# Last layer of a cross network: the sum of five output pairs made by an accumulating DMA onto seeded rows

## The chip, the cores and the metric

The kernel runs on one core of a Trainium2 chip. Its metric is the device time of one execution in microseconds (us), the median of repeated runs. Beside it stands one profiled execution, whose trace gives the start and length of every instruction. The engines are TensorE (PE; PEld is its weight load), VectorE (DVE), ScalarE (ACT), GpSimd (POOL) and SyncE (SP). SP, ACT and GpSimd can issue DMAs; a trailing q in a row (SPq, ACTq) means the engine's instruction queue.

## What is computed

```python
B, F, D, L = 4096, 26, 16, 6          # Din = 416
def reference(x0, ws, bs):            # x0: B x Din, ws: L x Din x Din, bs: L x Din, all bf16
    x = x0
    for l in range(ws.shape[0]):
        x = x0 * (x @ ws[l] + bs[l]) + x
    return x
```

Each of six layers multiplies the activations by a 416 x 416 matrix, adds a bias, multiplies by the first input x0 and adds the layer's own input x.

## The kernel before

Layers 0 to 4 work on transposed activations: features on the partitions (three full blocks of 128 in XM, the 32 that remain in XR, four groups of rows side by side), the 4096 rows along the free axis, in two halves s of 2048. For each tile TensorE sums in PSUM, ScalarE copies out and adds the bias (L146, L152), VectorE multiplies by x0 and adds x (L147, L148, L153, L154).

The last layer turns the roles round, so that its result comes out with rows on the partitions, as the output wants them. Its input is needed in that form too. XLrows holds it, 128 x 32 x 416: SP's DMA transposes (`xl_dmat`, L182) fill the 384 main columns, one for each half s and block of 128 features, as the tiles of layer 4 are finished; the 32 other columns go through scrR (L234) and two GpSimd copies (L235). X0rows holds x0 in the same form (L109).

The last layer has eight quads q (L269): q = 0 to 3 are in half s = 0, q = 4 to 7 in s = 1. A quad is four blocks of 128 rows, in two pairs h = 0 and 1; pair h has a PSUM tile of two blocks. `mm_q_full` (L281) gives 12 matmuls for a quad, `mm_q_rem` (L287, L290) the 32 remaining features and the bias. In odd quads but the last, the remainder comes last and closes both pairs together; in the others it comes first, and each pair closes with its own last matmul. PSUM has room for four such tiles.

For a pair, `ew_pair` (L293) copies PSUM into a t tile on ScalarE (L299), multiplies in place by X0rows on VectorE (L300), adds XLrows into an o tile on VectorE (L301) and stores 128 x 2 x 416 values, 208 KB, from SP (L302). The last quad's second pair is split into two single blocks, groups 2 and 3 (`ew_single`, L304 to L312), whose stores of 104 KB go out from ACT and from SP.

Two pools matter. t tiles come from `tpool`, four buffers used in turn (L41), by all layers; o tiles from `opool`, ten buffers (L42). An instruction that takes a buffer again waits for the last reader of what was in it, be that an engine or a DMA. Each engine runs its instructions in the order of its queue; a framework places the waits and may move an instruction forward or back in the queue when it builds the program. SP's queue carries, towards the end, the transposes into XLrows, then the output stores.

Of the kernel before, what the change touches and what calls it, by code (L numbers as in the profile page):

```python
# [10 lines left out]
ALU = mybir.AluOpType  # L11
BF16 = mybir.dt.bfloat16
# [4 lines left out]
def kernel(  # L17
# [7 lines left out]
    nc = tc.nc  # L25
    B, D = x0.shape
    L = ws.shape[0]
    P = 128
# [5 lines left out]
    CW = 512  # L34
# [6 lines left out]
    tpool = ctx.enter_context(tc.tile_pool(name="tpool", bufs=4))  # L41
    opool = ctx.enter_context(tc.tile_pool(name="opool", bufs=10))  # L42
# [3 lines left out]
    out_v = out.rearrange("(bt p) d -> p bt d", p=P)  # L46
# [12 lines left out]
    X0rows = big.tile([P, NBT, D], BF16)  # L59
    XLrows = big.tile([P, NBT, D], BF16)  # L60
# [117 lines left out]
    def new_pts():  # L178
        return [psum.tile([P, 2, CW], FP32, tag="ps", name=f"pt{h}") for h in range(2)]
# [89 lines left out]
    quads = [(s, i) for s in range(NS) for i in range(4)]  # L269
    NQ = len(quads)  # L270
# [7 lines left out]
    def mm_q_full(q, py, rem_first):  # L278
        for g in range(NG):
            for k in range(NK):  # L280
                nc.tensor.matmul(py[g // 2][:, g % 2, 0:D], lhsT=cur[:, k, q_cols(q, g)], rhs=WM[:, l, k, :],  # L281
                                 start=((not rem_first) and k == 0), stop=(rem_first and k == NK - 1))

    def mm_q_rem(q, py, rem_first):
        s, i = quads[q]
        for g in range(NG):
            nc.tensor.matmul(py[g // 2][:, g % 2, 0:D], lhsT=curR[32 * g:32 * g + 32, CW * s + 128 * i:CW * s + 128 * i + 128],  # L287
                             rhs=WR[32 * g:32 * g + 32, l, :], start=rem_first, stop=False, tile_position=(32 * g, 0))
        for g in range(NG):
            nc.tensor.matmul(py[g // 2][:, g % 2, 0:D], lhsT=ones[32 * g:32 * g + 1, :],  # L290
                             rhs=bLr[32 * g:32 * g + 1, :], start=False, stop=(not rem_first), tile_position=(32 * g, 0))

    def ew_pair(q, h, py):  # L293
        s, i = quads[q]
        b0 = 16 * s + 8 * h + i
        t = tpool.tile([P, 2 * CW], BF16, name="t")
        tv = t[:, 0:2 * D].rearrange("p (a d) -> p a d", a=2)
        o = opool.tile([P, 2, D], BF16, name="o")
        nc.scalar.copy(tv, py[h][:, :, 0:D])  # L299
        nc.vector.tensor_tensor(out=tv, in0=tv, in1=X0rows[:, b0:b0 + 5:4, :], op=ALU.mult)  # L300
        nc.vector.tensor_tensor(out=o[:], in0=tv, in1=XLrows[:, b0:b0 + 5:4, :], op=ALU.add)  # L301
        nc.sync.dma_start(out_v[:, b0:b0 + 5:4, :], o[:])  # L302

    def ew_single(q, g, py, eng):  # L304
        s, i = quads[q]
        b = 16 * s + 4 * g + i
        t = tpool.tile([P, 2 * CW], BF16, name="t")
        o = opool.tile([P, 2, D], BF16, name="o")
        nc.scalar.copy(t[:, 0:D], py[g // 2][:, g % 2, 0:D])
        nc.vector.tensor_tensor(out=t[:, 0:D], in0=t[:, 0:D], in1=X0rows[:, b, :], op=ALU.mult)  # L310
        nc.vector.tensor_tensor(out=o[:, 0, :], in0=t[:, 0:D], in1=XLrows[:, b, :], op=ALU.add)
        return lambda: eng.dma_start(out_v[:, b, :], o[:, 0, :])  # L312

    py = {0: new_pts()}
    mm_q_rem(0, py[0], True)
    for q in range(NQ):
        rem_first = (q % 2 == 0) or (q == NQ - 1)
        if q == NQ - 1:
            py[q] = new_pts()
            mm_q_rem(q, py[q], True)  # L320
        elif not rem_first:
            py[q] = new_pts()
        mm_q_full(q, py[q], rem_first)
        if not rem_first:
            mm_q_rem(q, py[q], False)
            if q + 1 < NQ - 1:
                py[q + 1] = new_pts()
                mm_q_rem(q + 1, py[q + 1], True)
        if q < NQ - 1:
            for h in range(2):  # L330
                ew_pair(q, h, py[q])
        else:
            ew_pair(q, 0, py[q])
            stores = [ew_single(q, 2, py[q], nc.scalar), ew_single(q, 3, py[q], nc.sync)]
            for st in stores:
                st()
# [30 lines left out]
```

## Time and profile before

| what | value |
|---|---|
| median of 3 runs | 135.62 us |
| the 3 runs | 134.5, 135.98, 135.62 us |
| the profiled execution's own time | 134.11 us |
| its span, first to last instruction | 132.3 us |
| mean granted TensorE clock | 0.993 |
| busy share of the span: PE, DVE, ACT, POOL | 94%, 80%, 63%, 5% |
| bytes read from and written to HBM | 6.23 MB, 3.41 MB |

The profiled execution's time is 1.8 us above its span (134.11 less 132.3), which is what lies around the first and the last instruction. A group's row names the line, engine, operation, output <- inputs, shape and count, then busy time in us and mean ns of one, then the engine's idle time before them and what ended it. A timeline row has start and length in us from the start of the span; a row with xN covers N such instructions.

### The profile page before, as it was taken

The numbers are of one execution on the slowest core, as the hardware profiler recorded it, in microseconds if no ns is written. First come the engines' busy times: TensorE is split into PE (matmuls) and PEld (weight loads), VectorE is DVE, ScalarE is ACT, GpSimd is POOL, SyncE is SP. The second block draws the span as 40 slices with busy tenths as digits, with TensorE's granted clock in tenths as the row PEclk, the third lists the DMA queues.
The fourth block names the chain that finished last, engine by engine and source line by source line (L and its number), as shares of the span: only waits on it lengthen the run. The fifth ranks groups of instructions, "written<-read, shape, count | busy, mean of one in ns | idle before, by whom it ended". The sixth has DMA issues, their size and how long they took to land.

```text
span 132.3 us, 2235 instructions
## 1 busy us (share of the span) xinstructions
PE 124.0 (94%) x847; PEld 51.5 (39%) x847; DVE 105.9 (80%) x180; ACT 83.1 (63%) x89; POOL 6.4 (5%) x18
## 2 busy tenths in 40 slices
PE   5799999999999999999999999999999999999920
PEld 2343343433334343434343434334434354554400
DVE  1013886989979898979898979898979999988990
ACT  0407484597849567848659756849565984584740
POOL 4011000420000000000000000000004100000000
PEclk9999999999999999999999999999999999999997
DMA  4999999999990000000000000000597899995453
GB/s 106 208 256 209 149 114 277 239 332 333 336 284 6 0 2 5 0 0 0 0 0 5 0 0 0 0 0 5 95 195 136 150 193 146 205 303 193 158 184 111
DMA packets 42095, 16.33 MB, mean 123 GB/s; under 512 B 30811, under 2 KB 42085, under 8 KB 42085
## 3 DMA queue, kind: packets, MB, share of 16 engines
q1 hardware_dynamic: 39272, 15.53, 52.5%
q10 hardware_dynamic: 2812, 0.67, 2.7%
q8 instruction: 6, 0.10, 0.3%
q14 instruction: 5, 0.03, 0.1%
HBM read 6.23 MB, written 3.41 MB: 73 GB/s over the span
## 4 chain that ended last, share of the span: by engine, by line
PE 83%; SPq 5%; DMA 3%; DVE 3%; issue 2%; ACT 1%; DVEq 0%
PE pt L159 48%; PE pt L281 10%; PE ph L193 9%; SPq L74 5%; PE pt L164 5%; PE pr L175 5%; DMA XM<-in_x_dram 3%; DVE t L300 2%; PE pr L170 2%; PE ph L210 2%; PE pt L287 1%; PE pt L290 1%; ACT t L299 1%; DVE o L301 1%; DVE t L310 0%
## 5 line engine op out<-in xcount | busy, mean ns | idle before, releaser
L159 PE MATMUL pt<-XM,WM 128*128 128x512 bf16 x288 | 65.1, 380 | 0.0
L146 ACT ACTIVATE t<-pt,bM 128x1024 bf16<-128x1024 f32 x48 | 49.6, 1115 | 19.6 <-PE pt L164 19.6
L147 DVE TENSOR_TENSOR t<-t,XM 128x1024 bf16<-128x1024 bf16 x60 | 41.7, 694 | 9.9 <-ACT t L146 9.3
L148 DVE TENSOR_TENSOR XM<-t,XM 128x1024 bf16<-128x1024 bf16 x60 | 41.7, 695 | 3.4
L159 PEld LDWEIGHTS <-WM 128*128 128x128 bf16 x288 | 26.8, 98 | 37.2 <-issue 7.2
L146 ACT ACTIVATE t<-ph,bM 128x1024 bf16<-128x1024 f32 x12 | 12.5, 1112 | 9.3 <-PE ph L210 9.3
L281 PE MATMUL pt<-WM,XM 128*128 128x416 bf16 x96 | 17.7, 340 | 0.0
L193 PE MATMUL ph<-XM,WM 128*128 128x512 bf16 x72 | 16.5, 379 | 1.0 <-DMA XM<-in_x_dram 0.8
L299 ACT CAST t<-pt 128x832 bf16<-128x832 f32 x15 | 12.2, 854 | 7.2 <-PE pt L290 5.2
L281 PEld LDWEIGHTS <-XM 128*128 128x128 bf16 x96 | 9.0, 98 | 8.4 <-issue 1.7
L193 PEld LDWEIGHTS <-WM 128*128 128x128 bf16 x72 | 6.8, 98 | 9.5 <-issue 2.0
L300 DVE TENSOR_TENSOR t<-t,X0rows 128x832 bf16<-128x832 bf16 x15 | 8.8, 585 | 0.9 <-ACT t L299 0.9
L301 DVE TENSOR_TENSOR o<-t,XLrows 128x832 bf16<-128x832 bf16 x15 | 8.9, 592 | 0.6
L152 ACT ACTIVATE t<-pr,bR 128x512 bf16<-128x512 f32 x10 | 6.5, 686 | 3.0 <-PE pr L175 2.6
L175 PE MATMUL pr<-XM,WM 128*32 128x512 bf16 x120 | 8.2, 379 | 0.0
L164 PE MATMUL pt<-XR,WR 32*128 32x512 bf16 x96 | 7.3, 379 | 0.0
L235 POOL COPY XLrows<-scrR 128x512 bf16<-128x512 bf16 x2 | 1.9, 962 | 73.8 <-DMA scrR<-XR 73.8
L154 DVE TENSOR_TENSOR XR<-t,XR 128x512 bf16<-128x512 bf16 x10 | 4.2, 423 | 0.7
L123 PE MATMUL wps<-warm 128*128 128x512 bf16 x8 | 3.3, 582 | 1.5 <-DVE dz L84 1.5
L96 ACT ACT_TABLE_LOAD x1 | 1.3, 1283 | 5.1 <-issue 5.1
L175 PEld LDWEIGHTS <-WM 128*32 128x32 bf16 x120 | 3.2, 97 | 2.6
L153 DVE TENSOR_TENSOR t<-t,XR 128x512 bf16<-128x512 bf16 x10 | 4.2, 416 | 0.0
(36 smaller groups left out, 29.7 us busy)
## 6 DMA issues: line engine op xcount, KB each, us to landing
X0rows<-in_x_dram SPq DMA_DIRECT2D x4, 832.0 KB, 11.3
out_dram<-o SPq DMA_DIRECT2D x15, 208.0 KB, 2.6
WM<-in_ws_dram SPq DMA_DIRECT2D x5, 312.0 KB
WR<-in_ws_dram SPq DMA_DIRECT2D x4, 130.0 KB, 4.2
WM<-in_ws_dram ACTq DMA_DIRECT2D x1, 312.0 KB
XM<-in_x_dram SPq DMA_TRANSPOSE x8, 5.0
xrem<-in_x_dram ACTq DMA_DIRECT2D x1, 128.0 KB, 5.8
xrem<-in_x_dram SPq DMA_DIRECT2D x1, 128.0 KB, 4.6
```

Source lines behind the costliest of these rows:

```text
L74: nc.sync.dma_start_transpose(out=XM[0][:, :, c0:c0 + CW], in_=x0[c0:c0 + CW, 0:NK * P])
L146: nc.scalar.activation(t[:], pt[:].rearrange("p a b -> p (a b)"), ACT.Identity, bias=bM[:, m, l:l + 1], scale=1.0)
L147: nc.vector.tensor_tensor(out=t[:], in0=t[:], in1=XM[0][:, m, c0:c0 + 2 * CW], op=ALU.mult)
L148: nc.vector.tensor_tensor(out=nxt[:, m, c0:c0 + 2 * CW], in0=t[:], in1=cur[:, m, c0:c0 + 2 * CW], op=ALU.add)
L159: nc.tensor.matmul(pts[g // 2][:, g % 2, :], lhsT=WM[:, l, k, 128 * m:128 * m + 128], rhs=cur[:, k, c0:c0 + CW], start=(first and k == 0), ...
L164: nc.tensor.matmul(pts[g // 2][:, g % 2, :], lhsT=WR[32 * g:32 * g + 32, l, 128 * m:128 * m + 128], rhs=curR[32 * g:32 * g + 32, CW * s:CW ...
L175: nc.tensor.matmul(pr[32 * g:32 * g + 32, :], lhsT=WM[:, l, k, NK * P:D], rhs=cur[:, k, c0:c0 + CW], start=False, stop=(k == NK - 1), tile ...
L193: nc.tensor.matmul(pt[m][:, gl, :], lhsT=WM[:, 0, k, 128 * m:128 * m + 128], rhs=cur[:, k, c0:c0 + CW], start=(k == 0), stop=False)
L281: nc.tensor.matmul(py[g // 2][:, g % 2, 0:D], lhsT=cur[:, k, q_cols(q, g)], rhs=WM[:, l, k, :], start=((not rem_first) and k == 0), stop=( ...
L299: nc.scalar.copy(tv, py[h][:, :, 0:D])
L300: nc.vector.tensor_tensor(out=tv, in0=tv, in1=X0rows[:, b0:b0 + 5:4, :], op=ALU.mult)
L301: nc.vector.tensor_tensor(out=o[:], in0=tv, in1=XLrows[:, b0:b0 + 5:4, :], op=ALU.add)
```

## The change

The five pairs (q, h) = (5, 0), (5, 1), (6, 0), (6, 1) and (7, 0) no longer get their add on VectorE. Their output rows are first filled with the layer's input: `seed_out` stores the pair's part of XLrows from SP, five stores, written in the code after the pairs of q = 3. When the pair's product t * X0rows is in the t tile, GpSimd issues a DMA from it that adds onto the output rows. Pair (7, 0) has its copy and multiply in two halves of 128 x 416 (`ew_split`). The other ten pairs and the two single blocks are as before. Matmuls, pools and the layers before are unchanged.

```diff
@@ ew_pair @@
         t = tpool.tile([P, 2 * CW], BF16, name="t")
         tv = t[:, 0:2 * D].rearrange("p (a d) -> p a d", a=2)
-        o = opool.tile([P, 2, D], BF16, name="o")
         nc.scalar.copy(tv, py[h][:, :, 0:D])
         nc.vector.tensor_tensor(out=tv, in0=tv, in1=X0rows[:, b0:b0 + 5:4, :], op=ALU.mult)
+        if (q, h) in by_dma:
+            nc.gpsimd.dma_start(out_v[:, b0:b0 + 5:4, :], tv, accum_op=ALU.add)
+            return
+        o = opool.tile([P, 2, D], BF16, name="o")
         nc.vector.tensor_tensor(out=o[:], in0=tv, in1=XLrows[:, b0:b0 + 5:4, :], op=ALU.add)
         nc.sync.dma_start(out_v[:, b0:b0 + 5:4, :], o[:])
+
+    def seed_out(q, h):
+        s, i = quads[q]
+        b0 = 16 * s + 8 * h + i
+        nc.sync.dma_start(out_v[:, b0:b0 + 5:4, :], XLrows[:, b0:b0 + 5:4, :])
+
+    def ew_split(q, h, py):
+        s, i = quads[q]
+        b0 = 16 * s + 8 * h + i
+        t = tpool.tile([P, 2 * CW], BF16, name="t")
+        for a in range(2):
+            nc.scalar.copy(t[:, a * D:a * D + D], py[h][:, a, 0:D])
+            nc.vector.tensor_tensor(out=t[:, a * D:a * D + D], in0=t[:, a * D:a * D + D], in1=X0rows[:, b0 + 4 * a, :], op=ALU.mult)
+        nc.gpsimd.dma_start(out_v[:, b0:b0 + 5:4, :], t[:, 0:2 * D].rearrange("p (a d) -> p a d", a=2), accum_op=ALU.add)
...
+    by_dma = [(q, h) for q in (NQ - 3, NQ - 2) for h in range(2)]
...
@@ loop over the quads @@
             for h in range(2):
                 ew_pair(q, h, py[q])
+            if q == NQ - 5:
+                for qq, h in by_dma + [(NQ - 1, 0)]:
+                    seed_out(qq, h)
         else:
-            ew_pair(q, 0, py[q])
+            ew_split(q, 0, py[q])
             stores = [ew_single(q, 2, py[q], nc.scalar), ew_single(q, 3, py[q], nc.sync)]
```

## The prediction

> **What bounds the kernel now.** I read the page first: its shares of the chain that ended last, then its groups and DMA rows. The chain is 83% TensorE, so up to the last layer every other engine hides behind the matmuls.
>
> ```profile
> span 132.3 us, 2235 instructions
> ...
> PE 83%; SPq 5%; DMA 3%; DVE 3%; issue 2%; ACT 1%; DVEq 0%
> ...
> L299 ACT CAST t<-pt 128x832 bf16<-128x832 f32 x15 | 12.2, 854 | 7.2 <-PE pt L290 5.2
> ...
> L300 DVE TENSOR_TENSOR t<-t,X0rows 128x832 bf16<-128x832 bf16 x15 | 8.8, 585 | 0.9 <-ACT t L299 0.9
> L301 DVE TENSOR_TENSOR o<-t,XLrows 128x832 bf16<-128x832 bf16 x15 | 8.9, 592 | 0.6
> ...
> L235 POOL COPY XLrows<-scrR 128x512 bf16<-128x512 bf16 x2 | 1.9, 962 | 73.8 <-DMA scrR<-XR 73.8
> ...
> out_dram<-o SPq DMA_DIRECT2D x15, 208.0 KB, 2.6
> ```
>
> The change touches only the end, so the chain in order of time comes next. TensorE carries it until 121.28; from there it goes ScalarE copy, then VectorE multiply, add, multiply, add to the end.
>
> ```profile
> 120.77 0.29 PE pt L287 x4
> 121.05 0.23 PE pt L290 x4
> 121.28 0.84 ACT t L299
> 122.13 0.02 issue
> 122.15 0.60 DVE t L300
> ```
>
> The timeline of the last 10 us has the times that everything below starts from (start, length).
>
> ```profile
> 121.27 2.37 ACT L299 CAST t<-pt 128x832 bf16<-128x832 f32 x3 [1.72 <-PE pt L290]
> ...
> 123.84 0.85 ACT L299 CAST t<-pt 128x832 bf16<-128x832 f32 x1 [0.20 <-PE pt L281]
> ...
> 125.46 0.85 ACT L299 CAST t<-pt 128x832 bf16<-128x832 f32 x1 [0.77 <-PE pt L281]
> ...
> 126.52 0.91 ACT L309 CAST t<-pt 128x416 bf16<-128x416 f32 x2 [0.20 <-PE pt L281]
> 126.67 0.58 DVE L300 TENSOR_TENSOR t<-t,X0rows 128x832 bf16<-128x832 bf16 x1
> 127.29 0.59 DVE L301 TENSOR_TENSOR o<-t,XLrows 128x832 bf16<-128x832 bf16 x1
> 127.80 0.65 DVE L310 TENSOR_TENSOR t<-t,X0rows 128x416 bf16<-128x416 bf16 x2
> 128.37 0.65 DVE L311 TENSOR_TENSOR o<-t,XLrows 128x416 bf16<-128x416 bf16 x2
> 128.77 0.38 ACTq L312 DMA_DIRECT2D out_dram<-o  x1
> 129.05 0.35 SPq L312 DMA_DIRECT2D out_dram<-o  x1
> ```
>
> The reader is to see that VectorE runs about one 1.13 us pair step after another while ScalarE has already finished (127.43). VectorE is late by some 0.8 us at the very end, and no more: with no adds ahead of them, the single multiplies could start when the last copies end. The last store, issued at 129.05, lands 1.8 us later (its own row), at 130.85, and the span ends 1.45 us after that.
>
> **The change part by part.** I write L for the time from the end of a multiply to the landing of its accumulating DMA, and g for the part of it in which GpSimd is occupied with the issue, since GpSimd issues the five one after the other.
>
> *Removed:* five adds of 592 ns on VectorE (2.96 us) and five SP stores. Of the 2.96 us only the lateness at the end is on the path. Without waits of any other kind, the last copy ends at 127.43, the multiply (368 ns) at 127.82, the add (368 ns, starting 0.07 later as in the rows) at 128.26, and SP stores at 128.29 instead of 129.05: a gain of 0.76 us. That is the ceiling of the change.
>
> *Added, seeds:* five SP stores of 208 KB from XLrows. In the built order they stand after the first two output stores, and the first waits for the last transposes into XLrows. The last of these is issued at 109.77 and a transpose of XLrows lands after 4.4 us, so at 114.2. Five issues at the slow pace of 0.757 us (the longest L302 row) end at 118.0; at 3.4 us (the slowest landing) the last lands by 121.4. Behind them wait the q1 to q3 stores, ready from 113.2 on; SP clears them at 0.45 us each (L302 at 115) before 122. The o pool has ten buffers, so VectorE waits for none of this. Cost 0; cover: the first accumulating DMA isn't ready before 122.74, and the first seed lands at about 117.6. If that cover of 5 us is gone, each us late is a us on the GpSimd queue.
>
> *Added, waits:* this decides. The t pool has four buffers. The pairs q5h0, q5h1, q6h0, q6h1 now hold one each until their DMA has landed, not until an add has read them. The built order shows the result: ScalarE's first q7h0 copy waits for the DMA of q5h0, the copy of group 2 for that of q5h1, the copy of group 3 for that of q6h0. Behind these copies stand all later ScalarE work (with its last store) and VectorE's last three multiplies and two adds.
>
> *L:* the trace has no GpSimd-issued DMA and no accumulating one, so both parts are bounded by the nearest rows. g: at least an SP issue, 0.37; at most, as an assumption, one 128x512 GpSimd copy, 0.96 (L235). The landing: at least a plain 208 KB store on a quiet queue, 2.1 (L302 at 123.4); at most a load followed by a store, since the destination must be read, then written: 4.6 (128 KB, xrem) + 2.1 = 6.7. So L lies between 2.47 and 7.66. I take 0.96 for g, because the one kind of GpSimd work seen near here has that length, and 3.4 for the landing: the slowest L302 store, when two 208 KB transfers lay in line, is nearest to one that moves the bytes twice. L = 4.36.
>
> *The sum with L = 4.36.* Multiplies of q5h0, q5h1, q6h0, q6h1 end at 122.74, 123.50, 124.25, 125.30 (copies end at 122.12, 122.88, 123.64, 124.69, and the adds between are gone). GpSimd starts at 122.78, 123.74, 124.70, 125.66; the DMAs land at 127.14, 128.10, 129.06, 130.02. ScalarE's q7h0 copy, free to run at 125.46 before, now starts at 127.19; its two halves take 0.91 (the L309 row, same shape), to 128.10; the second half's multiply ends at 128.49. GpSimd issues the fifth DMA at 128.54; it lands at 132.90. Meanwhile group 3's copy waits until 129.11, ends at 129.62, its multiply at 130.01, its add at 130.45, its store is issued at 130.48 and lands at 132.28. The later of the two, 132.90, plus 1.45 is 134.35: +2.05 on the span. L counts twice on this path, once in the wait and once in the last DMA: with the other terms kept, its change is 2L - 6.67, and that of group 3's store is L - 2.93.
>
> The profiled execution took 134.11 us and would take 136.2; the median of the three runs is 135.62, 1.5 us above it. On the median: 135.62 + 2.05 = 137.7 us.
>
> **A rule against a row.** Beside the two GpSimd copies of 101.04 to 102.95 two VectorE instructions took 0.91 and 1.09 us where the others of their lines took 0.69, so GpSimd work can slow VectorE; were the five issues to do so at the same rate, it would cost 0.1 to 0.2 us on a multiply of 0.37. In my sum the fourth issue ends at 126.62 and the multiplies on the path run after 127.7, so the term is 0 either way; with the quick landing below it would eat that much of the gain. The Trainium skill, SBUF — State Buffer, section "Who interferes with whom", says that a two-input VectorE instruction collides with a GpSimd instruction that reads SBUF and not with one that only writes, as descriptor generation does; by it this term is 0 in every case, and no run here shows it.
> The Trainium skill, DMA: Bandwidth & Descriptors, section "Anatomy of one DMA", fits a GpSimd-issued DMA as 2.0 us plus bytes over 436 GB/s: an estimate of 2.5 us for 208 KB, by which the sum would be -0.7 us; it speaks of plain copies, and the reading of the destination is not in it.
>
> **The rivals.**
> *Quick landing (other side, not slower).* L near its low end, 2.5: q5h0's DMA lands at 125.2, before the copy wants its buffer at 125.46; nobody waits; the fifth DMA, issued at 126.8, lands at 129.3, the last store at 130.1. That is the ceiling, -0.76 us: 134.9. For it: plain stores at this place land in 2.1. Against it: nothing plain reads its destination. It decides below L = 2.93, where group 3's path breaks even (the other does at 3.34); up to L = 3.8 the loss, 2L - 6.67 = 0.93, stays within what can be measured (136.6).
> *Slow accumulate.* L at 6 to 7.66: the copy starts at 128.8 to 130.5, and the last DMA, issued some 1.35 later, lands at 136.2 to 139.5: +5.3 to +8.7, 140.9 to 144.3. For it: loads in this trace take 4.6 us and more. Against it: those loads ran at the crowded start, and the queues near 125 are only half busy.
> *Seeds late.* The accumulating DMAs wait for their seeds. This decides once the first seed lands after 122.74. For it: the seeds wait for the transposes, which SP issues slowly (3.13 us for the last). Against it: the 5 us of cover. One us beyond the cover adds one to the forecast: 138.7.
>
> **How the numbers follow.** Forecast (L between 3.8 and 6, from +0.9 to +5.3, so 136.6 to 140.9): 0.55. Quick landing: 0.27. Slow accumulate: 0.13. Seeds late: 0.05. The bounds of L give 134.9 to 144.3; the range 134.8 to 141.5 leaves out most of the slow case and a little below. One per cent, 1.36 us, is about what a measurement can tell from no change here. The ceiling of 0.76 us is under it, so faster by over 1% needs the scatter of the runs as well (134.5 to 135.98): 0.05. Slower by over 1% needs L above about 4.0: most of the forecast, the slow case and the late seeds, 0.68. Within 1%: 0.27.
>
> **What would show it.** Right: ScalarE idle before the q7h0 copy, ended by a DMA into the output, copies starting near 127.2 and not 125.46; the last landing that of a GpSimd DMA; five GpSimd issues of about 1 us. Wrong: copies at 125.46 (L is short, take the quick case); last landing that of the SP store; GpSimd waiting for a seed; VectorE multiplies in this stretch well above 0.585 us; time lost before 121 us, where I expect no change.

## The result and the profile after

The change made the kernel slower: 139.95 us against 135.73 us for the kernel before (medians of four runs each), a ratio of 1.037 with a 95% interval of 1.031 to 1.043. I had forecast 137.7, so slower, but by 2.05 us where 4.2 were measured. In a second comparison, on the chip of experiments 1b, 5 and 7, it was 139.37 against 135.59, 1.028 (1.020 to 1.036). One run each of experiments 1 and 2 had TensorE's granted clock at 0.75 and a span of 167.5 and 164.5 us; the ratios leave them out, and the kernel of experiment 1, whose profile was that run, was run again as 1b.

The profiled execution took 140.25 us with a span of 138.2. From the page of the changed kernel:

```profile
span 138.2 us, 2228 instructions
...
q1 hardware_dynamic: 39272, 15.53, 52.0%
q0 software_dynamic: 1360, 1.07, 6.4%
...
L301 POOL DMA_DIRECT2D out_dram<-t x4 | 5.0, 1934 | 20.1 <-DMA out_dram<-o 20.1
...
out_dram<-XLrows SPq DMA_DIRECT2D x5, 208.0 KB, 2.3
out_dram<-t POOLq DMA_DIRECT2D x5, 208.0 KB, 5.8
```

The last row has the new thing: five DMAs issued by GpSimd, 5.8 us (median) from issue to landing, where plain stores before took 2.6. The queue row (packets, MB, share of 16 engines over the span) has a queue q0 that was not there. The 20.1 us of GpSimd's idle time is put down to a store; its queue's own events show that the seed was in by 119.9 and that GpSimd then waited for the multiply. In experiment 10, which has no seeds, the same row names the multiply (20.1 <-DVE t L299).

The timeline of the last 15 us of the changed kernel:

```profile
120.37 5.07 SPq L305 DMA_DIRECT2D out_dram<-o  x8
...
123.33 2.37 ACT L298 CAST t<-pt 128x832 bf16<-128x832 f32 x3 [1.72 <-PE pt L290]
...
124.21 0.59 DVE L299 TENSOR_TENSOR t<-t,X0rows 128x832 bf16<-128x832 bf16 x1 [0.49 <-ACT t L298]
...
125.11 5.04 POOL L301 DMA_DIRECT2D out_dram<-t  x4 [20.10 <-DMA out_dram<-o]
...
130.01 0.91 ACT L317 CAST t<-pt 128x416 bf16<-128x416 f32 x2 [3.26 <-DMA out_dram<-t]
...
131.63 1.20 POOL L319 DMA_DIRECT2D out_dram<-t  x1 [1.49 <-DVE t L318]
131.80 0.51 ACT L326 CAST t<-pt 128x416 bf16<-128x416 f32 x1 [0.88 <-DMA out_dram<-t]
...
132.92 0.51 ACT L326 CAST t<-pt 128x416 bf16<-128x416 f32 x1 [0.61 <-DMA out_dram<-t]
...
134.27 0.35 SPq L329 DMA_DIRECT2D out_dram<-o  x1
```

The three waits that the prediction named are all there, in its order: the q7h0 copy and the copies of groups 2 and 3 each end an idle stretch that "DMA out_dram<-t" released. The chain that ended last now runs through the same things:

```profile
126.68 6.16 DMA out_dram<-t
132.84 0.02 issue
132.86 0.02 ACTq L326
132.88 0.04 issue
132.92 0.51 ACT t L326
133.43 0.02 issue
133.45 0.39 DVE t L327
133.84 0.02 issue
133.86 0.38 DVE o L328
```

It is the DMA of (6, 0), issued at 126.68, 6.2 us long, then group 3's copy, multiply and add.

**What the two profiles can be compared on.** The spans differ by 5.9 us, more than the medians. Of that, 2.06 us is made ahead of the tail: the first copy of q5 starts at 121.27 in the one and 123.33 in the other. It goes back to the first matmuls. Nine of L193 took 2.10 us in the profile before and 4.00 in the profile after:

```profile
5.77 2.10 PE L193 MATMUL ph<-XM,WM 128*128 128x512 bf16 x9 [0.79 <-DMA XM<-in_x_dram]
```

```profile
6.17 4.00 PE L193 MATMUL ph<-XM,WM 128*128 128x512 bf16 x9 [0.82 <-DMA XM<-in_x_dram]
```

I take this for scatter, not for an effect of the change. Of the experiments' profiles, those of 2, 4, 8, 9, 10 and of the change again have these matmuls at 3.6 to 4.0 us, and those of 1b, 3, 5, 6 and 7 at 2.1; experiments 2, 4 and 8 have no GpSimd DMA at all. The runs of most kernels fall into two groups as well: those of the kernel before near 134.3 and 135.7. So I read all traces from the first q5 copy on, and times only by their intervals. A median also moves with the number of runs in each group. In the second comparison the change ran at 138.4 and 138.6 and at 140.1 and 140.5, the kernel before at 134.3 to 134.5 and at 135.5 to 136.1: within one group the change costs 4.1 to 4.5 us. The group of a run without a profile is read from its time alone, so such differences are argued, not shown.

### The profile page after: what moved, and what is told of

The parts are those of the page before. It is cut to its first block, busy times and chain, and to the rows that moved or that the text cites. A ratio compares the mean times of both kernels' runs of the same rounds, so it can differ in the third digit from the quotient of the medians.

```text
span 138.2 us, 2228 instructions
## 1 busy us (share of the span) xinstructions
PE 125.3 (91%) x836; PEld 52.0 (38%) x847; DVE 104.0 (75%) x176; ACT 83.2 (60%) x90; POOL 12.8 (9%) x23
## 3 DMA queue, kind: packets, MB, share of 16 engines
q0 software_dynamic: 1360, 1.07, 6.4%
## 5 line engine op out<-in xcount | busy, mean ns | idle before, releaser
L159 PE MATMUL pt<-XM,WM 128*128 128x512 bf16 x279 | 63.9, 380 | 0.9 <-issue 0.6
L193 PE MATMUL ph<-XM,WM 128*128 128x512 bf16 x70 | 18.2, 411 | 0.9 <-DMA XM<-in_x_dram 0.8
L298 ACT CAST t<-pt 128x832 bf16<-128x832 f32 x14 | 11.4, 854 | 6.4 <-PE pt L290 5.2
L193 PEld LDWEIGHTS <-WM 128*128 128x128 bf16 x72 | 7.1, 103 | 10.4 <-issue 3.8
L299 DVE TENSOR_TENSOR t<-t,X0rows 128x832 bf16<-128x832 bf16 x14 | 8.2, 587 | 1.7 <-ACT t L298 1.7
L301 POOL DMA_DIRECT2D out_dram<-t x4 | 5.0, 1934 | 20.1 <-DMA out_dram<-o 20.1
L304 DVE TENSOR_TENSOR o<-t,XLrows 128x832 bf16<-128x832 bf16 x10 | 5.9, 592 | 0.5
L115 POOL COPY WD<-WR 32x32 bf16<-32x32 bf16 (+1 forms) x8 | 3.1, 393 | 22.8 <-DMA WR<-in_ws_dram 22.6
```

Source lines behind the costliest of these rows:

```text
L159: nc.tensor.matmul(pts[g // 2][:, g % 2, :], lhsT=WM[:, l, k, 128 * m:128 * m + 128], rhs=cur[:, k, c0:c0 + CW], start=(first and k == 0), ...
L193: nc.tensor.matmul(pt[m][:, gl, :], lhsT=WM[:, 0, k, 128 * m:128 * m + 128], rhs=cur[:, k, c0:c0 + CW], start=(k == 0), stop=False)
L301: nc.gpsimd.dma_start(out_v[:, b0:b0 + 5:4, :], tv, accum_op=ALU.add)
```

## The experiments

In the table, "last store" and "end" are the start of the last SP store and the end of the span, both counted from the start of the first q5 copy, in us. The ratio is to the kernel before, measured beside it.

| kernel | median us | ratio (95%) | last store | end |
|---|---|---|---|---|
| before | | | 7.78 | 11.0 |
| the change | 139.95 | 1.037 (1.031 to 1.043) | 10.94 | 14.9 |
| the change again | 139.37 | 1.028 (1.020 to 1.036) | 11.31 | 15.4 |
| 1b own t buffers | 137.72 | 1.021 (1.014 to 1.027) | 7.30 | 14.4 |
| 2 plain SP stores | 135.98 | 1.005 (1.000 to 1.010) | 8.57 | 11.2 |
| 3 plain GpSimd stores | 136.48 | 1.011 (1.002 to 1.019) | 8.58 | 12.3 |
| 4 seeds alone | 135.17 | 0.998 (0.991 to 1.004) | 7.79 | 10.5 |
| 5 last pair only | 137.00 | 1.012 (1.006 to 1.018) | 7.48 | 12.7 |
| 6 without the last pair | 138.03 | 1.020 (1.012 to 1.029) | 10.87 | 14.5 |
| 7 q5 only, own buffers | 136.35 | 1.005 (1.000 to 1.009) | 7.47 | 11.9 |
| 8 no adds, no seeds | 135.07 | 1.000 (0.994 to 1.006) | 7.29 | 10.5 |
| 9 half of the last pair | 136.44 | 1.009 (1.003 to 1.015) | 7.89 | 11.7 |
| 10 no seeds | 138.84 | 1.021 (1.010 to 1.032) | 10.77 | 13.5 |

The theory: the q7 copies wait for t buffers that slow accumulating DMAs hold. The rivals: the accumulating DMAs set the end without any buffer; GpSimd's issuing is what is slow; the seeds crowd the queues; the time is lost ahead of the last layer.

**1 and 1b. Buffers of their own.**

```diff
+    dpool = ctx.enter_context(tc.tile_pool(name="dpool", bufs=5))
...
-        t = tpool.tile([P, 2 * CW], BF16, name="t")
+        t = (dpool if (q, h) in by_dma else tpool).tile([P, 2 * CW], BF16, name="t")
...
-        t = tpool.tile([P, 2 * CW], BF16, name="t")   # in ew_split
+        t = dpool.tile([P, 2 * CW], BF16, name="t")
```

> The change with a pool of five t buffers of its own for the five accumulating pairs, so that no copy waits for a DMA. Theory (the copies of q7 wait for buffers that the accumulating DMAs hold): q7's copies start as soon as TensorE has closed the pair, the last SP store goes out about 4 us sooner than in the change, and what ends the span is then the fifth accumulating DMA, queued behind the other four; 138.0 to 139.0 us. Rival (the accumulating DMAs set the end by themselves, the buffers do not matter): 139.9, as the change. Rival (the loss lies ahead of the last layer): 139.9 too, with the last rows of the timeline landing 3 us earlier but the start 2 us late.

The first measurement gave a ratio of 1.024 (1.012 to 1.035), too wide to decide. Expected of the second:

> The change with five t buffers of its own for the accumulating pairs, run again for an undisturbed profile. Theory (q7 waits for buffers that accumulating DMAs hold, and these land one behind the other): q7's first copy starts 4.2 us after the first q5 copy, as before the change, and not 6.7 us after it; the last SP store is issued some 7 us after that copy instead of 10.9; the end is then set by the fifth accumulating DMA, issued when GpSimd is through with the fourth and landing about 1.2 us after it; 2.0 to 2.5 us over the kernel before, so about 1.5 below the change. Rival (buffers do not matter): as the change, 3.8 to 4.2 over the kernel before.

From the timeline of experiment 1b:

```profile
121.53 2.37 ACT L299 CAST t<-pt 128x832 bf16<-128x832 f32 x3 [1.72 <-PE pt L291]
...
125.73 0.91 ACT L318 CAST t<-pt 128x416 bf16<-128x416 f32 x2 [0.77 <-PE pt L282]
...
127.35 2.24 POOL L320 DMA_DIRECT2D out_dram<-t  x1
...
128.83 0.35 SPq L330 DMA_DIRECT2D out_dram<-o  x1
```

and the answer on its line L320, the fifth DMA:

```profile
DMA to landing us min/median/max: 6.8/6.8/6.8
```

Without the wait the copy starts as soon as TensorE is done, 4.2 us after the q5 copy, and the last store goes out 3.6 to 4.0 us sooner than in the change. Yet the end moves by only 0.5 to 1.0 us: the fifth accumulating DMA, issued at 127.35, is behind the other four and lands at 134.15. So theory and first rival are both true: the wait and the queue of accumulating DMAs cost about the same, side by side, and taking away one uncovers the other. The median fell by 1.65 us, but three of the four runs, the profiled one with the quick start among them, lie at 137.6 to 137.7 and one at 139.3. Against the kernel before of the same group that is 3.3 and 3.5 us, 0.8 to 1.0 less than the change, which agrees with the trace.

**After again.**

> The change itself on the chip of the other runs, for a comparison in one place: 3.8 to 4.2 us over the kernel before if the loss is in the last layer. Rival (part of the gap of 6 us between the two profiles is made ahead of the last layer by the change): the first copy of q5 starts 2 us later than in the kernel before in each run; if the early difference is scatter of the start, it differs from profile to profile of the same kernel.

3.8 us over the kernel before on the median, and the early rows as in the first profile; that they are scatter is argued from the other kernels that show them too.

**6. Without the fifth DMA.** `by_dma` and its four seeds stay, pair (7, 0) is done by `ew_pair` as before:

```diff
-                for qq, h in by_dma + [(NQ - 1, 0)]:
+                for qq, h in by_dma:
...
-            ew_split(q, 0, py[q])
+            ew_pair(q, 0, py[q])
```

> The change with the four accumulating DMAs of q5 and q6 and the four shared t buffers, but pair (7, 0) copied, multiplied, added and stored as before. Theory (the wait for buffers sets the end through group 3, whose copy waits for the DMA of (6, 0)): the last SP store is issued 10.5 to 11.3 us after the first q5 copy, as in the change (10.9 and 11.3), and the time is that of the change within 0.5 us, 3.5 to 4 over the kernel before. Rival (the fifth DMA sets the end): 1 to 2 us below the change.

From its timeline, group 3's copy with its wait, and the last store:

```profile
130.59 0.51 ACT L326 CAST t<-pt 128x416 bf16<-128x416 f32 x1 [0.81 <-DMA out_dram<-t]
...
132.10 0.35 SPq L329 DMA_DIRECT2D out_dram<-o  x1
```

The last store goes out at 10.87, as expected, and the end is 14.5, 0.4 to 0.9 sooner than in the change. The median is 2.6 over the kernel before, 1.3 below the change, less than I expected; by the trace alone it is 3.4. All four runs lie at 137.6 to 138.1, the profiled one with the quick start, so by their times they are all of the quick group; its runs of the kernel before lie at 133.9 to 134.4, and against these it is 3.8, as expected. The waits do carry the end by themselves.

**2, 3 and 8. What the DMA costs.** In experiment 2 the five DMAs are plain stores from SP, in 3 plain stores from GpSimd; in 8 plain SP stores without seeds and with the buffers of experiment 1. All three leave the layer's input out of the rows of these pairs. The line in `ew_split` is changed in the same way.

```diff
-            nc.gpsimd.dma_start(out_v[:, b0:b0 + 5:4, :], tv, accum_op=ALU.add)
+            nc.sync.dma_start(out_v[:, b0:b0 + 5:4, :], tv)       # experiments 2 and 8
+            nc.gpsimd.dma_start(out_v[:, b0:b0 + 5:4, :], tv)     # experiment 3
```

> The change with the five accumulating DMAs replaced by plain stores of the product from SP; the seeds, the four shared t buffers and the waits for a buffer stay; the add of the layer's input is left out for these rows. Theory (the length of the accumulating DMA makes the buffer wait): a plain store lands in 2 to 3 us, nobody waits long, 135.0 to 135.7 us, about 0.7 below the kernel before. Rival (holding buffers for any DMA costs the time): 138 or more. Rival (seeds or the order of stores cost the time): 137 or more.

> The change with the five DMAs still issued by GpSimd but without the accumulation, plain stores of the product; the add of the layer's input is left out for these rows. If the reading and adding in the DMA is what takes long: landing near 2.5 us from issue and about 136 to 137 us. If issuing from GpSimd is what takes long (1.2 us each, one behind the other, and its start): 138.5 to 139.9 us with landings of 4 us and more.

> The ceiling: five t buffers of their own, no seeds, and the products of the five pairs stored by plain SP stores; the add of the layer's input is left out for these rows. Theory: VectorE is late by 0.5 to 0.8 us in the kernel before and by nothing here, so the last SP store is issued 7.0 to 7.3 us after the first q5 copy instead of 7.8, and the time is 0.3 to 0.8 us below the kernel before: no way to do these adds elsewhere can bring more. Rival (the last 10 us are bound by VectorE throughout, 2.96 us of adds): 2 us or more below.

The queue row and the DMA issues on the page of experiment 3, and the q7h0 copy in its timeline:

```profile
q0 software_dynamic: 400, 1.07, 2.6%
...
out_dram<-t POOLq DMA_DIRECT2D x5, 208.0 KB, 3.5
...
127.25 0.91 ACT L317 CAST t<-pt 128x416 bf16<-128x416 f32 x2 [2.29 <-DMA out_dram<-t]
```

The same five transfers, from the same engine, without the add. Against the page of the changed kernel: 400 packets in place of 1360, that is 80 a DMA in place of 272, and 2.6% of 133.8 us, 0.70 us of all 16 DMA engines for each, in place of 6.4% of 138.2, 1.77 us. The issues took 0.73 us each (the first 0.84) in place of 1.20 to 2.47, and the landing 3.5 in place of 5.8. So the accumulation, not GpSimd, is the slow part: the last store is 3.2 to 3.5 us later than before in the change, and 0.8 later with plain DMAs from either engine.

The 0.8 in experiment 2 contradicts my "nobody waits long": the q7h0 copy waits 2.29 us for a DMA there too, as in experiment 3. Its stores from line L301, and those of experiment 8 from line L302:

```profile
DMA to landing us min/median/max: 3.5/3.6/3.7
```

```profile
DMA to landing us min/median/max: 2.1/2.1/2.1
```

With seeds a plain store takes 3.6 us, without them 2.1: the seeds shift eight stores into the stretch in which the products go out (SP was issuing them until 125.4 in the changed kernel). Experiment 8 also gives the ceiling: with the five adds left out altogether the last store is 0.49 us sooner, and the time cannot be told from that of the kernel before (within one group of runs, as sorted by their times, it is 0.4 and 0.7 us less).

**4 and 10. The seeds.** Experiment 4 adds the seeds to the kernel before, which then stores over them (the five pairs are written out there); experiment 10 is the change without `seed_out`'s calls, so the layer's input is missing from these rows.

```diff
+            if q == NQ - 5:     # added in 4, taken away in 10
+                for qq, h in by_dma + [(NQ - 1, 0)]:
+                    seed_out(qq, h)
```

> The kernel before with the five seed stores added at the place where the change has them; the five pairs are then stored as before, over the seeds. Theory: the seeds are covered, 135.6 to 136.2 us. Rival (the seeds hold up SP and its stores, which the tail then waits for): 137 to 138 us.

> The change without its five seed stores: the DMAs add onto whatever the output rows hold, so the layer's input is missing from these rows; everything else stays. Theory (the accumulating DMA itself is slow, the seeds only push plain stores into its way): the first accumulating DMA lands 4.0 to 4.6 us after its issue, the third near 6; the last SP store is issued 10.0 to 10.7 us after the first q5 copy (10.9 and 11.3 in the change), 0.3 to 1 us below the change. Rival (the backlog that the seeds make on the queues is the larger part, as plain stores that land in 3.5 us with seeds and 2.1 us without suggest): the first lands in 3.4 us, the last store goes out 9.5 us after the copy, 1.5 to 2 us below the change.

The seeds alone cost nothing that can be measured. Without them the first accumulating DMA lands in 4.0 us instead of 4.8, but the last store still goes out at 10.77: the rival's 9.5 is excluded. The end, though, is 13.5, 1.4 to 1.9 us sooner than in the change: the last store goes out 0.2 to 0.5 sooner, lands in 1.7 instead of 2.1 and 2.3, and the end follows 1.1 us after the landing instead of 1.8, for which no run shows the reason. Within one group of runs it is 3.1 to 3.4 us over the kernel before, about 1 us less than the change. So the seeds, which cost nothing alone, seem to cost about 1 us beside the accumulating DMAs. On the medians, 138.84 against 139.37 from different chips, this cannot be seen.

**5 and 9. One accumulating DMA, and half of one.** In 5 `by_dma` is empty, so only (7, 0) is added by a DMA; in 9 its group 1 goes through VectorE and SP as well.

```diff
-    by_dma = [(q, h) for q in (NQ - 3, NQ - 2) for h in range(2)]
+    by_dma = []
...
-        nc.gpsimd.dma_start(out_v[:, b0:b0 + 5:4, :], t[:, 0:2 * D].rearrange("p (a d) -> p a d", a=2), accum_op=ALU.add)
+        nc.gpsimd.dma_start(out_v[:, b0, :], t[:, 0:D], accum_op=ALU.add)     # experiment 9 only
```

> The change with the accumulating DMA for pair (7, 0) alone; q5 and q6 get their adds on VectorE as before, so no buffer is held when a copy wants one. Theory: one accumulating DMA on a quiet queue lands 4.1 us after its issue (the fifth of the change); VectorE is through with q6 at 126.75 on the clock of the profile before, the two half multiplies end near 127.5, the DMA is issued at 127.8 and lands at 131.9, against 130.85 before: +1.0 us. Rival (only crowded accumulating DMAs are slow): lands in 2.5 us, the last SP store ends the span, -0.5 us.

> One accumulating DMA of half the size (104 KB, group 0 of the last quad); group 1 is added on VectorE and stored from SP, all else as before. If the landing of a lone accumulating DMA (4.8 us for 208 KB) is mostly paid by row: 3.2 to 3.9 us. If it is mostly fixed: 4.4 us or more. The time lies between that of the kernel before and 1.3 us above it.

The DMA issues of experiments 5 and 9:

```profile
out_dram<-t POOLq DMA_DIRECT2D x1, 208.0 KB, 4.8
...
out_dram<-o SPq DMA_DIRECT2D x1, 104.0 KB, 3.4
```

```profile
out_dram<-t POOLq DMA_DIRECT2D x1, 104.0 KB, 3.2
```

A lone accumulating DMA is slow too, 4.8 us, and it ends the span of experiment 5 (issued 127.91, landing 132.71; the span is 134.2): +1.6 us by the trace, +1.4 by the median, where I expected +1.0. Half the bytes take 1.6 us less, so most of the length is paid by the row; if it is linear, some 1.6 us remain fixed. The plain store issued beside it took 3.4 us to land, against 1.8 in the kernel before.

**7. Early pairs only.** `by_dma` holds the two pairs of q5, with buffers of their own; q6 and q7 are as before.

```diff
-    by_dma = [(q, h) for q in (NQ - 3, NQ - 2) for h in range(2)]
+    by_dma = [(q, h) for q in (NQ - 3,) for h in range(2)]
```

> Accumulating DMAs for the two pairs of q5 alone, with buffers of their own; q6 and q7 as in the kernel before. Theory: the DMAs land within 7 us of the multiplies, so by 129.8 on the clock of the profile before, ahead of the last store; VectorE is spared two adds, 1.18 us, of which the 0.76 us of its lateness counts: -0.7 us against the kernel before. Rival (accumulating DMAs slow VectorE or the stores beside them): 0 or above.

The miss: not -0.7 us but +0.76 on the median, +0.5% (0.0 to 0.9); it is 0.8 within each group of runs too. The last store goes out 0.31 us sooner than before, but lands in 2.6 us instead of 1.8, and the end follows 1.8 us after the landing instead of 1.45. No version found beats the kernel before.

## Why the prediction went wrong

Its direction and its mechanism held, and 139.95 lies inside the range that it gave; it failed on size, 4.2 us in place of 2.05. On the clock of the profile before (times after less 2.06):

| step | predicted | measured |
|---|---|---|
| multiply of q5h0 to GpSimd's start | 0.04 us | 0.31 us |
| from one GpSimd start to the next (q5, q6) | 0.96 us | 0.84, 0.73, 0.99 us |
| GpSimd starts the DMA of (6, 0) at | 124.70 | 124.62 |
| landing from GpSimd's start, q5 and q6 | 4.36 us each (0.96 + 3.4) | 4.8, 5.8, 6.2, 6.3 us |
| the same, fifth DMA | 4.36 us | 4.1 us |
| DMA of (5, 0) lands at | 127.14 | 127.85 |
| DMA of (6, 0) lands at | 129.06 | 130.78 |
| fifth DMA lands at | 132.90 | 133.7 |
| last SP store lands at | 132.28 | 134.3 |
| landing to end of span | 1.45 us | 1.8 us |

The answer on line L301 of the changed kernel, the DMAs of q5 and q6:

```profile
L301 POOL DMA_DIRECT2D out_dram<-t x4: 1327/1970/2468, 125.1 to 127.7; - x4
...
DMA to landing us min/median/max: 4.8/6.0/6.3
```

*The step that failed* is "I take 0.96 for g ... and 3.4 for the landing": one length, 4.36 us from GpSimd's start, for all five, so that only GpSimd's issuing spaced them. GpSimd was not late. Its issues took 1.33 to 2.47 us, but their rows overlap, and each began 0.3 to 0.4 us after its multiply. The landing was too short: the first took 4.8 us, 0.4 more, and those behind it were held up by one another as well. The four were issued 0.84, 0.73 and 0.99 us apart and landed 1.8, 1.1 and 1.1 us apart, so the third was 6.2 us under way. That put the DMA of (6, 0) 1.72 us later than in the sum, and with it group 3's copy and the last store. The store itself landed in 2.1 instead of 1.8, and the end came 0.35 later after it: 132.28 + 1.72 + 0.3 + 1.8 is 136.1, against the 134.35 of my sum. These are the 1.8 us by which the trace exceeds it (3.84 against 2.05, both from the first q5 copy on).

*The row I chose.* The slowest plain store, 3.4, stood for a DMA that "moves the bytes twice". Experiment 3 shows that 3.5 (3.8 for the first) is what a plain store takes at that place; the adding comes on top, 1.0 us for the first in line (4.8 less 3.8) and 2.3 on the median (5.8 less 3.5). The 3.4 was counted from the start of an issue already, so with g in front of it the sum held part of an issue twice, which hid part of the miss. The bounds, 2.1 and 6.7, did hold all landings but two of experiment 1b (7.0 and 6.8).

*Which path ends.* I had the fifth DMA last by 0.6 us; group 3's store was last, by 0.6, which the prediction had listed as a sign of being wrong.

*Removed adds.* The ceiling of 0.76 us is 0.5 in experiment 8, and no more; VectorE's 2.96 us of adds were nearly all covered, as said.

*Seeds at nothing.* Right for the seeds by themselves (experiment 4), wrong beside the accumulating DMAs, where the end comes 1.4 to 1.9 us sooner in the trace without them (experiment 10), and wrong in what it hid: the seeds started at 117.77 (115.7 on the clock before, not 114.2), the stores behind them were issued until 123.4 and not cleared "before 122", and a plain store among them takes 3.6 us and not 2.1. The quick rival, which rested on 2.1, was therefore not open to this change, even had the adding been free.

*The rule on ports.* VectorE's multiplies beside the GpSimd issues took 0.59 us each, 0.585 before. The Trainium skill, SBUF — State Buffer, section "Who interferes with whom", expects no collision with descriptor generation, and this agrees. The fit in DMA: Bandwidth & Descriptors, section "Anatomy of one DMA", 2.5 us as an estimate for 208 KB, is met by the last plain GpSimd store of experiment 3, on a quiet queue: 2.5 us. For an accumulating one 4.0 to 4.9 us were measured alone or first in line.

*What stays open:* how much of the lone accumulating DMA's length is the reading of the output rows and how much the adding, and why it goes in 272 packets (in the trace 256 of 832 bytes, one for each output row, and 16 of 4 bytes) where the plain one has 80; no run separates these. No run takes away the shared buffers and the fifth DMA together with all four others kept. That the start's two speeds are independent of the kernel is argued from which kernels show them, not from a run that controls it.

## What to carry to other kernels

Before moving an add into a DMA, ask what the engine's add was worth on the path (here 0.5 us of 2.96), and price the DMA as a queue: several in a row hold one another up, here landing 1.1 to 1.8 us apart, and each holds its source buffer until it has landed, not until an engine has read it. An operation that the trace lacks should be bounded in length and in throughput, both. Where two new waits run side by side, undoing one shows only their difference; undo each, and then both.

## What the runs showed of the hardware

- An accumulating 208 KB DMA onto HBM rows of 832 bytes took 272 packets, whose times add up to 1.77 us of all 16 DMA engines, the plain one from GpSimd 80 packets and 0.70 us. Landing: 4.0 to 4.9 us alone, first in line or (the fifth) issued after a pause of 3 us and more, 4.9 to 7.0 issued right behind others; plain 2.1 (SP) and 2.5 (GpSimd) on a quiet queue.
- GpSimd's queue took 0.73 us for a plain issue (0.84 for the first) and 1.20 to 1.33 for an accumulating one (up to 2.5 when issued back to back, with the rows overlapping), and began 0.3 to 0.4 us after the multiply that it waited for.
- A 104 KB store from SP beside accumulating DMAs landed in 2.6 to 4.3 us (experiments 7, 5, 1b), in 1.8 without them.
- The first matmuls ran at one of two speeds (nine in 2.10 or in 3.6 to 4.0 us), with GpSimd DMAs in the kernel or without; everything after is 1.1 to 2.1 us later in the profiles with the slow ones.
